# All products with v of a group in one run: a change to the order of work in an attention and experts kernel

## The chip, the cores and the metric

The kernel runs on one core of one Trainium2 chip. Times are device microseconds of one execution; the time before is the median of three runs. One core has a matrix engine (TensorE, PE in profiles), a vector engine (VectorE, DVE), a scalar engine (ScalarE, ACT), a general engine (GpSimd, POOL) and a queue that issues transfers (SyncE, SP). Each works through its own instructions in order, and they wait for each other by semaphores.

## The reference

Attention with hashed buckets, then a layer of eight experts. For 4 batches and 8 heads, 768 tokens and 64 dimensions a head:

```python
q_bits = (np.einsum('bhsd,dk->bhsk', q, proj) > 0)     # 6 bits: a token's bucket; k the same
mask = q_bucket[:, :, :, None] == k_bucket[:, :, None, :]
scores = scale * np.matmul(q, k.transpose(0, 1, 3, 2))
scores = np.where(mask, scores, -1000000000.0)
attn = softmax(scores)
x = (attn @ v), heads side by side, one row of 512 per token      # 3072 rows
expert_idx = np.argmax(x @ w_gate, axis=1)
for e in range(8):                                       # each token goes to one expert
    out[mask_e] = gate_w * (np.maximum(x[mask_e] @ w1[e], 0.0) @ w2[e])
```

All is float32. The experts' products are written as three products of rounded parts.

## The kernel before, in words

**Pairs, groups, blocks, steps.** Two heads of a batch make a pair: 16 pairs, four to a batch (`pr`, `NPAIR`). A pair has two groups (`g`) of three tiles of 128 queries. A block is one tile of queries of one head, 128 x 768 scores; a group has six, in the order of `blocks` (L522). The main loop (L773) has one step per block, 192 in all, and `n = i % 6` is the step's place in its group. I count the places as first to sixth step. Groups with `g == 0` are called even, those with `g == 1` odd.

**What a step holds.** Step i issues the scores of block i + 2 (L805: four products on TensorE into one of two score buffers, then on VectorE one pass at L241 that clips and takes the row maximum) and the exponentials of block i + 1 (ScalarE, L249 and L250). The scores of block i + 2 can start when the row maximum of block i is done, since there are two buffers.

**Two ways to turn a block.** A product with v needs the block turned. In pairs 1 to 13, the first, third and fifth block of a group go out to DRAM in pieces after the exponentials (`move`, L253: four writes, two steps later one read) and are turned by VectorE six steps later (L266, `turns`, at the very start of the step). The second, fourth and sixth block are turned by six transposes on TensorE (`transposes`, L270) into two banks of the pool `ps_t`, and two copies on ScalarE (L278) bring them to `pt`. This stands in the step after the block's own (`between`, L558).

**Products with v.** `av` (L288) is 24 products of 128 columns (12 in the program; each runs as two) for one tile of queries: both heads, six blocks of keys. For the group before (`prev`) it is called in the second, fourth and sixth step, once each (L839 and L840). After the third call ScalarE takes the sums out of PSUM (`av_evac`, L296, the copy at L300) in the next step, and two steps later `out_and_route` (L744) follows: VectorE's reciprocal (L308), three transposes on TensorE back to rows (L323) into the bank `misc` and VectorE's scaling (L324).

**Routing.** After a batch's last pair, pieces follow in the list `light`, one to a step: `logits` (L341: eight products with the gate's weights into `misc`, and a copy by ScalarE, L348), `gather_heads` (L352: three transposes into `misc`, L356, and five VectorE operations), `one_hot` (L366: five VectorE operations, those at L367 to L371 reading `misc`), `ranks` (L373: eight small products into `misc`, L376 to L381, and VectorE at L382 to L386) and `rows` (L388: two VectorE operations and three row scatters by GpSimd). This falls into the groups that begin pairs 4, 5, 8, 9, 12 and 13, and the odd ones between. The pool `ps_m` holds one bank, `misc`; it is also used by the codes of the next pair (`pair_codes`, L141, in the fourth step of an even group: eight products, L146, VectorE at L148, GpSimd at L149). Whoever writes it next waits until the last reader is done.

**Order.** `manual_schedule` (L758) keeps TensorE, VectorE, ScalarE and SP in the order in which the program issues them; `in_turn` does it for most of GpSimd's work. There is no planner: the loop's order is the order on each engine. `PREPARE` (L549) says in which step the next pair's operands are made: keys in the first step of an even group, codes and queries in the fourth, the codes' write to DRAM in the fifth; the codes come back in the first step of the odd group (L780).

**After the attention** come the experts (L921 to L1139), eight in turn, where weights are read, rounded and multiplied. The change doesn't touch them.

Of the kernel before, what the change touches and what calls it, by code (L numbers as in the profile page):

```python
# [8 lines left out]
F32 = mybir.dt.float32  # L9
# [9 lines left out]
P = 128  # L19
B, H, S, D = 4, 8, 768, 64  # L20
NB = S // P
NPAIR = H // 2
# [36 lines left out]
def lsh_attention_moe_kernel(ctx, tc, qkd, q2d, k2d, v, pjbd, wg, w1, w2, ident_in, tri_in, cols_in, eoff_in, ids_in, out):  # L59
    nc = tc.nc  # L60
    V, A, G, PE, SY = nc.vector, nc.scalar, nc.gpsimd, nc.tensor, nc.sync
# [223 lines left out]
    late = []  # L285
# [10 lines left out]
    def av_evac(pr, g, sums, o, defer):  # L296
        b, pi = divmod(pr, NPAIR)
        ot = otp.tile([P, 384], F32, name="ot")
        if defer:
            late.append(lambda: A.copy(out=ot, in_=o[:, 0:384]))  # L300
# [29 lines left out]
    def route(b, g):  # L330
# [8 lines left out]
        slot = gp.tile([P, 3, 1], I32, name="slot")  # L339

        def logits():  # L341
            lps = ps_t.tile([P, 512], F32, name="t") if (b, g) == (B - 1, 0) else ps_m.tile([P, 512], F32, name="misc")
            for pi in range(NPAIR):
                PE.matmul(out=lps[32 * pi:32 * pi + 32, 0:384], lhsT=wg_sb[:, pi, :], rhs=ots[(b, g, pi)], start=True, stop=True)
            if (b, g) == (B - 1, 0):
                V.tensor_copy(out=lsb, in_=lps[:, 0:384])
            else:
                A.copy(out=lsb, in_=lps[:, 0:384])  # L348
# [39 lines left out]
        def rows():  # L388
            x = xrows[(b, g)]
            V.reduce_max(out=slot, in_=pos, axis=AX.X)  # L390
            V.reciprocal(out=x[:, :, :, SEG + 1], in_=mx[:, :, 1:2].broadcast_to([P, 3, NG]))
            for jj in range(3):
                ins = G.indirect_dma_start(out=xs, out_offset=bass.IndirectOffsetOnAxis(ap=slot[:, jj, :], axis=0),
                                           in_=x[:, jj].rearrange("p g w -> p (g w)"), in_offset=None)
                rows_apart("xs", ins)
                if jj == 0 and b + 1 < B:
                    in_turn(ins)
            if not g and b + 1 < B:
                light.pop(0)()

        return [logits, gather_heads, one_hot, pause, ranks, rows] if b + 1 < B else [logits, gather_heads, one_hot, ranks, rows]

    def last_route(sums, o):

# [114 lines left out]
    NPR = B * NPAIR  # L519
# [26 lines left out]
    for hh in range(2):  # L546
# [2 lines left out]
    PREPARE = (  # L549
        {(0, 1): [(pair_codes, ())], (0, 2): [(codes_out, ())], (0, 3): [(k_operands, (0,))], (0, 4): [(q_operands, (0,))],  # L550
         (0, 5): [(q_operands, (1,)), (codes_back, ())], (1, 0): [(k_operands, (1,))]},
        {(0, 0): [(k_operands, (0,)), (k_operands, (1,))], (0, 3): [(pair_codes, ()), (q_operands, (0,)), (q_operands, (1,))],
         (0, 4): [(codes_out, ())]})

    def moved_block(k):
        return k % 6 in MOVES.get(steps[k][:2], ())

    def between(k):  # L558
        return 0 < k < len(steps) - 1 and moved_block(k - 1) and moved_block(k + 1)
# [18 lines left out]
    def run_expo(i):  # L578
        pr, g, jj, hh = steps[i]
        moves = moved_block(i)  # L580
        p = expo(*soft.pop(i), sums_of(pr, g), 2 * jj + hh)
        if moves:
            out, back, turn = move(p, partial(probs_t, pr, g, jj), hh)
            later.append((i, out))
            returns.append((i + 2, back))
            turns.append((i + 6, turn))
        else:
            probs[i] = p

# [16 lines left out]
    def pick_first(rows):  # L606
# [15 lines left out]
        return [counts, rows, pause, pause, pause, most, which]  # L622

    def pause():
        pass
# [118 lines left out]
    def out_and_route(pr, g):  # L744
        while divide:
            divide.pop(0)()
        if pr % NPAIR < NPAIR - 1:
            av_out(pr, g)
            return

        pieces = route(pr // NPAIR, g)
        pieces[0]()
        light.append(lambda: av_out(pr, g))
        light.extend(pieces[1:])
        if (pr, g) == (NPR - NPAIR - 1, 1):
            light.extend(pick_first(light.pop()))
# [13 lines left out]
    SY.dma_start(out=h0[0][:, 384:S], in_=q2d[0][:, 384:S])  # L770
    CLEARS = (1, 1, 2, 3, 4, 6, 8, 10)
    prev, due, extra = None, [], {}
    for i, (pr, g, jj, hh) in enumerate(steps):  # L773
        n = i % 6
        while turns and turns[0][0] == i:
            turns.pop(0)[1]()
        while later and later[0][0] <= i:
            later.pop(0)[1]()
        if (g, n) == (1, 0) and 0 < pr < NPR - 2 or (pr, g, n) == (NPR - 2, 0, 5):
# [23 lines left out]
                prefill(e)  # L803
        if i + 2 < len(steps):
            run_scores(i + 2)  # L805
        if 2 <= i < 4:
# [9 lines left out]
        while late:  # L816
            late.pop(0)()
# [4 lines left out]
        side = (g, n) == (0, 3) and 0 < pr < NPR - 1  # L822
        if due and due[0][0] == i and not last:
            due.pop(0)[1]()
        elif light and not side and (not last or n < 2):
            light.pop(0)()
        if not last:
            for f, x in PREPARE[min(pr, 1)].get((g, n), ()) if pr + 1 < NPR else ():
                f(pr + 1, *x)
        for k in (i - 1, i):  # L830
            if k in probs and (k < i or not between(k)):
                pk, gk, jk, hk = steps[k]
                transposes(probs.pop(k), probs_t(pk, gk, jk)[:, hk], (A, A))

        if prev is not None:
            if n == 0:
                o = ps_o.tile([P, 512], F32, name="o")
            order_p = blocks(prev[0], prev[1])[1]
            for jp in (order_p[:2], order_p[2:])[n] if last and n < 2 else order_p[n // 2:n // 2 + 1] if not last and n % 2 == 1 else ():  # L839
                av(prev[0], prev[1], jp, o)  # L840
            if n == (1 if last else 5):
                av_evac(prev[0], prev[1], prev[2], o, (prev[0], prev[1]) != (NPR - 2, 1) and not last)
                if not last:
# [410 lines left out]
```

## Time and profile before

| | |
|---|---|
| median of three runs | 714.4 us (709.75 to 717.0) |
| profiled execution | 719.9 us, span of its instructions 718.1 us |
| TensorE products busy | 696.8 us, 97% of the span |
| VectorE busy | 484.8 us, 68% |
| ScalarE busy | 439.1 us, 61% |
| GpSimd busy | 408.8 us, 57% |
| granted TensorE clock, mean | 0.992 |
| chain that ended last: TensorE 51%, time without a visible wait | 24% |
| pairs 1 to 13 in the profiled execution | about 33 to 356 us from the start |

How to read it: busy time of TensorE includes products that overlap, so a high share says that the engine has no holes, not that it works at its peak. A share over the whole span mixes the attention (up to about 415 us) with the experts; the stretches of single groups say more. The scores of a group start two steps ahead, so a stretch that starts with a group's first scores and ends with the next group's first scores lies two steps before the group in the program.

### The profile page before, as it was taken

How to read it: one execution, taken by the hardware profiler on the slowest of the kernel's cores; microseconds unless marked ns; L12 is line 12 of the kernel's file. 1: busy time of each engine (PE TensorE's matmuls, PEld its weight loads, DVE VectorE, ACT ScalarE, POOL GpSimd, SP SyncE). 2: the span in 40 equal slices, each digit the busy share in tenths (PEclk: the TensorE clock that was granted, in tenths of full speed). 3: DMA queues.
4: the chain of work that ended last, by engine and by line, in shares of the span. 5: the costliest groups of instructions: out<-in, count | busy, mean ns of one | idle time of the engine just before them, and what ended most of it. 6: DMA issues, size and time to landing. Idle time of an engine off the chain costs nothing.

```text
span 718.1 us, 16099 instructions
## 1 busy us (share of the span) xinstructions
PE 696.8 (97%) x5735; PEld 615.9 (86%) x5735; DVE 484.8 (68%) x1012; ACT 439.1 (61%) x996; POOL 408.8 (57%) x410
## 2 busy tenths in 40 slices
PE   7999999999999999999999989999999999999996
PEld 3888887788888888888888869999999999988994
DVE  6667878878778877878787656746464656464641
ACT  6887887788887888877777642434343434334330
POOL 3895757686656866676684320056564654707171
PEclk9999999999999999999999999999999999999999
DMA  8989878989988899799886217474746476665421
GB/s 279 294 258 283 276 232 254 290 261 278 281 260 259 250 291 266 235 289 287 230 251 185 89 62 184 118 196 119 196 135 180 145 208 160 207 163 158 147 70 47
DMA packets 110082, 150.34 MB, mean 209 GB/s; under 512 B 12548, under 2 KB 77990, under 8 KB 109992
## 3 DMA queue, kind: packets, MB, share of 16 engines
q1 hardware_dynamic: 105016, 136.52, 65.6%
q0 software_dynamic: 4976, 12.69, 5.0%
q8 instruction: 47, 0.77, 0.4%
q14 instruction: 43, 0.35, 0.1%
HBM read 94.23 MB, written 55.18 MB: 208 GB/s over the span
## 4 chain that ended last, share of the span: by engine, by line
PE 51%; issue 24%; POOL 13%; DMA 6%; DVE 2%; SPq 1%; ACT 1%; POOLq 0%; another core or an unknown queue 0%; DVEq 0%; ACTq 0%
PE o L293 17%; PE s L232 11%; POOL y L1029 11%; PE s L233 9%; PE t L275 9%; PE misc L146 2%; PE misc L323 2%; POOL yo L1027 2%; DMA y<-yo,tok 2%; DMA xr<-xs 1%; DVE p L241 1%; DMA qk<-qkd 1%; PE s L732 1%; DMA wraw<-w 1%; ACT p L250 1%
## 5 line engine op out<-in xcount | busy, mean ns | idle before, releaser
L232 PE MATMUL s<-k,q 128*128 128x512 f32 (+1 forms) x384 | 149.4, 389 | 0.1
L293 PE MATMUL o<-pt,vt 128*64 128x128 f32 x2304 | 146.8, 277 | 0.0
L293 PEld LDWEIGHTS o<-pt,vt 128*64 128x64 f32 x2304 | 123.8, 137 | 23.5 <-issue 18.4
L241 DVE TENSOR_SCALAR_CACHE_REDUCE p<-s 128x768 f32<-128x768 f32 x111 | 106.0, 955 | 35.9 <-PE s L233 31.6
L278 ACT COPY pt<-t 128x384 f32<-128x384 f32 x222 | 95.7, 482 | 52.6 <-PE t L275 46.0
L233 PE MATMUL s<-c 76*128 76x512 f32 (+1 forms) x384 | 124.1, 344 | 0.0
L1029 POOL DMA_INDIRECT y<-yo,tags x88 | 100.4, 1141 | 24.9 <-issue 22.7
L250 ACT ACTIVATE p<-p,m 128x768 f32<-128x768 f32 x111 | 104.4, 941 | 9.4 <-DVE m L244 6.7
L241 DVE TENSOR_SCALAR_CACHE_REDUCE pd<-s 128x768 f32<-128x768 f32 x81 | 76.8, 948 | 33.1 <-PE s L233 11.0
L232 PEld LDWEIGHTS s<-k,q 128*128 128x128 f32 x384 | 73.3, 191 | 27.6 <-issue 14.8
L987 ACT ACTIVATE hh<-hps 128x352 fp32r<-128x352 f32 (+3 forms) x56 | 27.9, 500 | 105.1 <-PE hps L1001 88.0
L275 PE MATMUL t<-ident,p 128*128 128x128 f32 x666 | 92.0, 274 | 0.1
L266 DVE STREAM_TRANSPOSE pt<-pq 128x768 f32<-128x768 f32 x81 | 78.6, 970 | 14.1 <-DMA pq<-moved 11.7
L701 DVE TENSOR_TENSOR wlo<-wraw,whi 128x1024 fp32r<-128x1024 f32 x60 | 72.9, 1217 | 17.4 <-ACT whi L696 15.7
L233 PEld LDWEIGHTS s<-c 76*128 76x128 f32 x384 | 74.0, 193 | 9.2 <-ACT c L208 0.4
L1020 PE MATMUL hps<-hh,whi 128*128 128x448 f32 (+9 forms) x224 | 77.3, 345 | 2.0 <-ACT whi L696 2.0
L275 PEld LDWEIGHTS t<-ident,p 128*128 128x128 f32 x666 | 75.2, 141 | 4.5 <-issue 2.5
L250 ACT ACTIVATE pd<-pd,m 128x768 f32<-128x768 f32 x81 | 75.9, 937 | 5.2 <-DVE m L244 0.8
L1020 PE MATMUL hps<-hh,wlo 128*128 128x436 f32 (+6 forms) x224 | 77.2, 344 | 1.8 <-DVE wlo L701 1.4
L1027 POOL TENSOR_TENSOR yo<-yt,tags 128x512 f32<-128x512 f32 (+3 forms) x25 | 23.2, 950 | 97.3 <-DVE yt L1022 97.2
L1020 PE MATMUL hps<-hl,whi 128*128 128x436 f32 (+6 forms) x224 | 77.1, 344 | 0.0
L1001 PE MATMUL hps<-xh,whi 128*128 128x352 f32 (+3 forms) x224 | 75.2, 336 | 0.0
(226 smaller groups left out, 1284.0 us busy)
## 6 DMA issues: line engine op xcount, KB each, us to landing
wraw<-w SPq DMA_DIRECT2D x64, 512.0 KB
moved<-pd SPq DMA_DIRECT2D x324, 96.0 KB
pq<-moved SPq DMA_DIRECT2D x81, 384.0 KB
qk<-qkd SPq DMA_DIRECT2D x30, 384.0 KB
xs<-zrow SPq DMA_DIRECT2D x8, 910.0 KB
vt<-v SPq DMA_DIRECT2D x16, 384.0 KB
coded<-cr SPq DMA_DIRECT2D x15, 192.0 KB
c<-coded SPq DMA_DIRECT2D x30, 72.0 KB
```

The costliest lines, as they stand in the source:

```text
L232: PE.matmul(out=s[:, c0:c1], lhsT=q1[:, qs], rhs=k1[:, c0:c1], start=True, stop=False)
L233: PE.matmul(out=s[:, c0:c1], lhsT=q2[0:KM, qs], rhs=k2[0:KM, c0:c1], start=False, stop=True)
L241: V.tensor_scalar(out=to, in0=of, scalar1=-0.5 * BIG, scalar2=None, op0=ALU.max, op1=ALU.max, accum_out=m[:, 0:1])
L250: A.activation(p, p, AF.Exp, bias=m[:, 1:2], scale=0.125, accum_out=sums[:, idx:idx + 1])
L266: V.transpose(out=pt()[:, hh].rearrange("p c (s j) -> p c s j", j=SQ), in_=q.rearrange("p s c i -> p c s i"))
L275: PE.transpose(out=t[:, i * P:i * P + P], in_=p[:, kc * P:kc * P + P], identity=ident)
L278: A.copy(out=dst, in_=src)
L293: PE.matmul(out=o[hh * D:hh * D + D, jj * P:jj * P + P], lhsT=vt[:, kc, hh * D:hh * D + D], rhs=pt[:, hh, kc], start=kc == 0, stop=kc == N ...
L701: loeng.tensor_tensor(out=lo[:, i:i + step], in0=cell["t"], in1=bf(hi[:, i:i + step]), op=ALU.subtract)
L1001: PE.matmul(out=hps[:, 0:w], lhsT=wt[:, c, fs], rhs=xt[:, c, 0:w], start=n == 0, stop=n == 3 * NDC - 1)
L1020: PE.matmul(out=yps[:, 0:w], lhsT=wt[:, f, ds], rhs=ht[:, 0:w], start=n == 0, stop=n == 3 * NFC - 1)
L1029: rows_apart("out", G.indirect_dma_start(out=out_seg, out_offset=bass.IndirectOffsetOnAxis(ap=tags[:, i, 0:1].bitcast(I32), axis=0), in_=y ...
```

## The change

In the groups from pair 1, first group, to pair 13, second group (`together`), the three calls of `av` for the group before all stand in the sixth step, behind that step's scores. Around that:

- The turnings on TensorE move: the second block's from the third to the fourth step, the fourth block's from the fifth step to the first of the next group, the sixth block's from the first step of the next group to its third, there in front of the step's exponentials (`turned_at`, `turn_ready`).
- VectorE turns the third block one step later, in the fourth step of the next group, behind that step's row maximum (`behind`).
- The sums leave PSUM one step later (second step instead of first).
- `pair_codes` and the queries' operands move from the fourth to the third step of an even group, the codes' write from the fifth to the fourth.
- `out_and_route` moves from the second step to the fourth. The routing pieces get fixed places (`lay_out`), counted from the step of the products with v: `logits` 3 later (third step), the scaled rows 4 (fourth), `gather_heads` 6 (sixth), `one_hot` 8 (second of the next group), `ranks` 11 (fifth), `rows` 12 (sixth). `logits` now always takes a bank of `ps_t` instead of `misc`. The steps of `pick_first`, which finds the first expert, follow 12, 16 and 17 later.

```diff
-            lps = ps_t.tile([P, 512], F32, name="t") if (b, g) == (B - 1, 0) else ps_m.tile([P, 512], F32, name="misc")
+            lps = ps_t.tile([P, 512], F32, name="t")
...
-        {(0, 0): [(k_operands, (0,)), (k_operands, (1,))], (0, 3): [(pair_codes, ()), (q_operands, (0,)), (q_operands, (1,))],
-         (0, 4): [(codes_out, ())]})
+        {(0, 0): [(k_operands, (0,)), (k_operands, (1,))], (0, 2): [(pair_codes, ()), (q_operands, (0,)), (q_operands, (1,))],
+         (0, 3): [(codes_out, ())]})
...
+    def together(pr, g):
+        return (0, 1) < (pr, g) < (NPR - 2, 0)
+
+    def turned_at(k):
+        pr, g = steps[k][:2]
+        if together(pr, g) and (pr, g) != (NPR - 3, 1):
+            return k + {1: 2, 3: 3, 5: 3}[k % 6]
+        return k + between(k)
...
-            turns.append((i + 6, turn))
+            behind = i % 6 == 2 and together(pr, g) and (pr, g) != (NPR - 3, 1)
+            turns.append((i + 6 + behind, behind, turn))
...
+    def lay_out(i, pr, g):
         if pr % NPAIR < NPAIR - 1:
-            av_out(pr, g)
+            pieces.setdefault(i + 4, []).append(lambda: out_and_route(pr, g))
             return
...
+        logits, gather_heads, one_hot, ranks, rows = route(pr // NPAIR, g)
+        way = [(3, logits), (4, lambda: out_and_route(pr, g)), (6, gather_heads), (8, one_hot), (11, ranks)]
...
+            way.append((12, rows))
+        for n, f in way:
+            pieces.setdefault(i + n, []).append(f)
...
+    def turn_ready(i):
+        for k in sorted(probs):
+            if turned_at(k) <= i:
+                pk, gk, jk, hk = steps[k]
+                transposes(probs.pop(k), probs_t(pk, gk, jk)[:, hk], (A, A))
...
             run_scores(i + 2)
+        while turns and turns[0][0] == i:
+            turns.pop(0)[2]()
...
+        if together(pr, g) and n == 2:
+            turn_ready(i)
         if i + 1 < len(steps):
             run_expo(i + 1)
...
-        for k in (i - 1, i):
-            if k in probs and (k < i or not between(k)):
-                pk, gk, jk, hk = steps[k]
-                transposes(probs.pop(k), probs_t(pk, gk, jk)[:, hk], (A, A))
+        for f in pieces.pop(i, ()):
+            f()
+        turn_ready(i)
...
+            joined = together(pr, g)
+            if n == (5 if joined else 0):
                 o = ps_o.tile([P, 512], F32, name="o")
...
+            elif joined:
+                now = order_p if n == 5 else ()
+            else:
+                now = order_p[n // 2:n // 2 + 1] if n % 2 else ()
+            for jp in now:
                 av(prev[0], prev[1], jp, o)
```

## Rows read from the trace of the kernel before

**Rows 1.** Windows: length, busy of PE, PEld, DVE, ACT, POOL, clock, DMA share, GB/s.

```profile
180.51:192.86 12.35, 12.35 (x127) 10.21 (x125) 9.98 (x19) 10.79 (x26) 7.52 (x8) 1.00 0.95 298
192.86:204.41 11.55, 11.55 (x119) 10.06 (x117) 8.86 (x18) 9.23 (x26) 7.99 (x8) 1.00 0.87 240
204.41:244.68 40.27, 39.58 (x408) 32.16 (x406) 33.01 (x84) 31.94 (x82) 26.27 (x26) 1.00 0.88 263
```

**Rows 2.** TensorE's timeline, ordinary odd group: start us, duration us, line, operation, count.

```profile
192.86 0.50 PE L232 MATMUL s<-k,q 128*128 128x512 f32 x1
...
193.68 0.82 PE L275 MATMUL t<-ident,p 128*128 128x128 f32 x6
194.25 0.48 PE L232 MATMUL s<-k,q 128*128 128x512 f32 x1
...
195.12 1.53 PE L293 MATMUL o<-pt,vt 128*64 128x128 f32 x24
196.59 0.50 PE L232 MATMUL s<-k,q 128*128 128x512 f32 x1
```

**Rows 3.** Costliest groups of instructions: count | busy us, mean ns | idle before.

```profile
L293 PE MATMUL o<-pt,vt 128*64 128x128 f32 x2304 | 146.8, 277 | 0.0
```

**Rows 4.** TensorE's timeline at the start of pair 1: scores directly behind scores.

```profile
38.29 0.40 PE L232 MATMUL s<-k,q 128*128 128x512 f32 x1
...
39.00 0.50 PE L323 MATMUL misc<-ident,ot 128*128 128x128 f32 x3
```

**Rows 5.** TensorE's timeline in a group that routes.

```profile
127.32 0.30 PE L376 MATMUL misc<-run,ident 128*128 128x24 f32 x2
...
127.61 0.86 PE L275 MATMUL t<-ident,p 128*128 128x128 f32 x6
...
129.36 0.52 PE L323 MATMUL misc<-ident,ot 128*128 128x128 f32 x3 [0.18 <-DVE mx L386]
...
132.09 0.49 PE L356 MATMUL misc<-ident,lsb 128*128 128x128 f32 x3
132.42 0.82 PE L275 MATMUL t<-ident,p 128*128 128x128 f32 x6
```

**Rows 6.** VectorE's timeline in the ordinary odd group.

```profile
193.96 0.96 DVE L241 TENSOR_SCALAR_CACHE_REDUCE pd<-s 128x768 f32<-128x768 f32 x1 [0.75 <-issue]
...
196.21 0.97 DVE L266 STREAM_TRANSPOSE pt<-pq 128x768 f32<-128x768 f32 x1
...
199.08 0.96 DVE L241 TENSOR_SCALAR_CACHE_REDUCE p<-s 128x768 f32<-128x768 f32 x1 [0.43 <-PE s L233]
...
199.96 0.18 DVE L308 RECIPROCAL inv<-sums 128x6 f32<-128x6 f32 x1
200.25 0.56 DVE L324 TENSOR_TENSOR xr<-misc,inv 128x384 f32<-128x384 f32 x1
```

**Rows 7.** TensorE's timeline in pair 14: codes, then transposes, then products with v.

```profile
366.10 0.85 PE L146 MATMUL misc<-qk,pj 128*32 128x384 f32 x8
366.88 0.88 PE L275 MATMUL t<-ident,p 128*128 128x128 f32 x6
367.69 0.55 PE L293 MATMUL o<-pt,vt 128*64 128x128 f32 x6
```

**Rows 8.** ScalarE's timeline in the ordinary odd group: two copies of a turned block.

```profile
194.21 0.86 ACT L278 COPY pt<-t 128x384 f32<-128x384 f32 x2 [1.12 <-PE t L275]
```

**Rows 9.** VectorE's timeline in two groups that route: one-hot and ranks.

```profile
122.00 0.18 DVE L367 TENSOR_TENSOR misc<-misc,mx 128x24 f32<-128x24 f32 x1
...
122.76 0.17 DVE L371 TENSOR_TENSOR lg<-misc,mx 128x24 f32<-128x24 f32 x1
...
128.48 0.18 DVE L382 TENSOR_TENSOR pos<-misc,ohb 128x24 f32<-128x24 f32 x1
...
129.06 0.16 DVE L386 TENSOR_SCALAR mx<-misc 128x3 f32<-128x3 f32 x1
```

**Rows 10.** VectorE's timeline: the longest wait for moved data.

```profile
309.62 0.98 DVE L266 STREAM_TRANSPOSE pt<-pq 128x768 f32<-128x768 f32 x1 [2.12 <-DMA pq<-moved]
```

More of the change, by code (lines that the diff above doesn't have):

```diff
@@ L294, in av, with av_evac @@
                           start=kc == 0, stop=kc == NB - 1)
-    def av_evac(pr, g, sums, o, defer):
+    def av_evac(pr, g, sums, o, defer, i):
         b, pi = divmod(pr, NPAIR)
@@ L299, in av_evac @@
         if defer:
-            late.append(lambda: A.copy(out=ot, in_=o[:, 0:384]))
+            late.append((i, lambda: A.copy(out=ot, in_=o[:, 0:384])))
         else:
@@ L397, in rows @@
                     in_turn(ins)
-            if not g and b + 1 < B:
-                light.pop(0)()
-        return [logits, gather_heads, one_hot, pause, ranks, rows] if b + 1 < B else [logits, gather_heads, one_hot, ranks, rows]
+        return [logits, gather_heads, one_hot, ranks, rows]
     def last_route(sums, o):
@@ L620, in which @@
             V.tensor_scalar(out=best_i, in0=best[:, 1:2], scalar1=-1.0, scalar2=float(E), op0=ALU.mult, op1=ALU.add)
-        return [counts, rows, pause, pause, pause, most, which]
-    def pause():
-        pass
+        return counts, most, which
     def number(tile_1):
@@ L746, in out_and_route @@
             divide.pop(0)()
+        av_out(pr, g)
+    pieces = {}
+    def lay_out(i, pr, g):
         if pr % NPAIR < NPAIR - 1:
-            av_out(pr, g)
+            pieces.setdefault(i + 4, []).append(lambda: out_and_route(pr, g))
             return
[L751 to L754, printed above, removed]
+        logits, gather_heads, one_hot, ranks, rows = route(pr // NPAIR, g)
+        way = [(3, logits), (4, lambda: out_and_route(pr, g)), (6, gather_heads), (8, one_hot), (11, ranks)]
         if (pr, g) == (NPR - NPAIR - 1, 1):
-            light.extend(pick_first(light.pop()))
+            counts, most, which = pick_first(rows)
+            way += [(12, counts), (12, rows), (16, most), (17, which)]
+        else:
+            way.append((12, rows))
+        for n, f in way:
+            pieces.setdefault(i + n, []).append(f)
     in_order.enter_context(tc.manual_schedule(engines={PE.engine, V.engine, A.engine, SY.engine}))
@@ L772, in lsh_attention_moe_kernel @@
     prev, due, extra = None, [], {}
+    def turn_ready(i):
[3 more added lines that the diff above has]
+                transposes(probs.pop(k), probs_t(pk, gk, jk)[:, hk], (A, A))
     for i, (pr, g, jj, hh) in enumerate(steps):
         n = i % 6
-        while turns and turns[0][0] == i:
-            turns.pop(0)[1]()
+        while turns and turns[0][:2] == (i, False):
+            turns.pop(0)[2]()
         while later and later[0][0] <= i:
@@ L805, in lsh_attention_moe_kernel @@
             run_scores(i + 2)
+        while turns and turns[0][0] == i:
+            turns.pop(0)[2]()
         if 2 <= i < 4:
@@ L815, in lsh_attention_moe_kernel @@
             in_turn(G.tensor_copy(out=run, in_=eoff[:, 1]))
-        while late:
-            late.pop(0)()
+        while late and late[0][0] <= i:
+            late.pop(0)[1]()
         sums = sums_of(pr, g)
@@ L821, in lsh_attention_moe_kernel @@
         last = pr == NPR - 1 and g == 1
-        side = (g, n) == (0, 3) and 0 < pr < NPR - 1
         if due and due[0][0] == i and not last:
             due.pop(0)[1]()
-        elif light and not side and (not last or n < 2):
+        elif light and (not last or n < 2):
             light.pop(0)()
@@ L829, in lsh_attention_moe_kernel @@
                 f(pr + 1, *x)
-        for k in (i - 1, i):
-            if k in probs and (k < i or not between(k)):
-                pk, gk, jk, hk = steps[k]
-                transposes(probs.pop(k), probs_t(pk, gk, jk)[:, hk], (A, A))
+        for f in pieces.pop(i, ()):
+            f()
+        turn_ready(i)
         if prev is not None:
-            if n == 0:
+            joined = together(pr, g)
+            if n == (5 if joined else 0):
                 o = ps_o.tile([P, 512], F32, name="o")
             order_p = blocks(prev[0], prev[1])[1]
-            for jp in (order_p[:2], order_p[2:])[n] if last and n < 2 else order_p[n // 2:n // 2 + 1] if not last and n % 2 == 1 else ():
+            if last:
+                now = (order_p[:2], order_p[2:])[n] if n < 2 else ()
+            elif joined:
+                now = order_p if n == 5 else ()
+            else:
+                now = order_p[n // 2:n // 2 + 1] if n % 2 else ()
+            for jp in now:
                 av(prev[0], prev[1], jp, o)
             if n == (1 if last else 5):
-                av_evac(prev[0], prev[1], prev[2], o, (prev[0], prev[1]) != (NPR - 2, 1) and not last)
-                if not last:
+                av_evac(prev[0], prev[1], prev[2], o, (prev[0], prev[1]) != (NPR - 2, 1) and not last,
+                        i + 1 + (joined and pr < NPR - 3 + (not g)))
+                if joined:
+                    lay_out(i, prev[0], prev[1])
+                elif not last:
                     due.append((i + 2, lambda a=prev[0], c=prev[1]: out_and_route(a, c)))
```

## The prediction

> **What bounds the kernel now.** I read the table of engines first: TensorE is busy for 97% of the span, so the question is whether it is the bound in the pairs that change. The windows answer it [rows 1]: in an ordinary even group (one with the codes of the next pair) TensorE is busy for 12.35 of 12.35 us, in an ordinary odd one for 11.55 of 11.55, while VectorE and ScalarE have 1.6 to 2.7 us left. The three groups after a batch's end, which route, take 40.27 us, 39.58 of them busy. So a saving on TensorE counts in full as long as nobody else comes late, and each wait put into its queue counts in full too. Then I read TensorE's timeline for what a switch costs [rows 2]. A scores run takes 0.82 us from its first product to the first transpose, 0.87 to the first product with v; six transposes take 0.57; a run with v of 24 products takes 1.47 until the next scores start. Its busy time is 1.53 and a product lasts 0.28 in the mean [rows 3], so its 24 starts are spread over about 1.26 us, 55 ns apart, and 0.21 is the way out.
>
> **The change, term by term.** All is for a group in pairs 1 to 13 (26 groups).
>
> Joining the three runs: 72 products are 71 x 0.055 + 0.21 = 4.10 us instead of 3 x 1.47 = 4.41: 0.31 less. Two entries of 0.87 become 0.82: 0.10 less. Scores directly behind scores, now in the third and the sixth step, start faster: 0.71 instead of 0.82 [rows 4], twice: 0.22 less. Nothing longer than 24 products stands in the trace; the bounds for a longer run's spacing are 55 ns and, without overlap, 0.28 us, and I take 55, the run's own. In "TensorE: Matmul & The Clock Gate", section "Back-to-back issue gap", the Trainium skill gives about 81 ns for each 128-column product that comes with its own weight load. By that the run would take 72 x 0.081 = 5.8 us, 1.7 more than by the row; the trace contradicts it for 24 in a row.
>
> An ordinary odd group is then, by steps: 0.82 + 0.57; 0.82; 0.71 + 0.57; 0.82 + 0.33 (the three transposes that bring rows back, from 132.09 to 132.42, [rows 5]) + 0.57; 0.82; 0.76; 4.10. Sum 10.89. One wait comes in: the scores of the fourth step need the bank whose row maximum starts 1.10 after its own scores [rows 2, 6], at 2.48, lasts 0.96 and frees TensorE 0.14 later from 129.06 + 0.16 to 129.36, [rows 5, 9], at 3.58 against 3.49. So 10.98, against 11.55: **0.57 less, in 10 groups**. An even one has the codes besides, now behind transposes: 0.78 for the eight products and 0.24 because transposes before such narrow products take 0.81 instead of 0.57 [rows 7]; with the fourth scores that much later, the wait of 0.09 is gone. So 11.91, against 12.35: **0.44 less, in 7 groups**. Together 5.7 + 3.1 = 8.8 us.
>
> Do the others keep up? VectorE, counted from the group's first scores: maximum at 4.66 (I take 1.08, a little under the row's 1.10, behind scores that follow transposes and start at 3.58), turning, reciprocal, scaling, turning, two maxima, turning, at 0.88 (maximum) or 0.89 (turning, 0.97 less an overlap of 0.08) each and 0.29 + 0.56 for the pair [rows 6]: done at 10.8, and the next group's first maximum starts at 10.98 + 1.10 = 12.08. So VectorE is hidden with 1.2 us to spare; the last turned block, done near 8.2, is needed by the last third of the long run near 9.4. ScalarE's 9.23 us [rows 1] fit in 10.98. SP issues the same transfers in the same order, with the codes' write one step earlier; if POOL hasn't weighed them by then, the next block's four writes queue behind it. POOL's key and query preparations and its row scatters keep their order and have 3.5 us or more of gaps [rows 1]. Those moves I cost at nothing: ScalarE still spreads the exponentials that start the transfers about evenly, and the third block's turning comes a step later than it did. If that cover is gone it is the second rival. One distance shrinks: the codes return in an odd group's first step and are read by the fifth step's scores, 7.8 us after the group's first scores until now (1.39 + 2.34 + 1.39 + 2.70), 5.3 then (3.58 + 0.82 + 0.33 + 0.57). No row shows their landing; the cost is between nothing and the whole 2.5 us in 13 pairs. TensorE never waited for them so far, so I take nothing, and count the other end to the slow side of the range.
>
> **Where it is given back: the groups that route.** The routing pieces share one PSUM bank ("misc") with the codes and with the rows' transposes, and TensorE stops at each of them until VectorE has read the last tenant. The new layout puts the pieces on TensorE next to its bare, short steps (0.82 us each), where VectorE is behind: the maximum, then the turning that now follows it, then reciprocal and scaling. From the start of the fourth step's scores, the scaling ends at 1.08 + 0.88 + 0.89 + 0.29 + 0.56 = 3.70 [rows 6], and TensorE may write the bank at 3.84.
> - First routing group (even): the logits' products, eight of the codes' shape, add 0.78, so the fourth scores start at 5.29. TensorE gets to the heads' transposes in the sixth step 3.25 us later (0.82 + 0.33 + 0.57 + 0.82 + 0.71) and waits 0.59. With 0.38 for them and 4.10 for the run: 13.61.
> - Second (odd): the logits now take a bank of the transposes. The block's transposes start at 2.92, their copies 0.53 later at the earliest (193.68 to 194.21), half of 0.86 + 0.08 for the first [rows 2, 8]: a wait of at least 0.25 past 3.73, and about 0.8 if an exponential still runs in front. ScalarE then has an exponential and the evacuation before it, so I take 0.55, between the two: logits at 4.28, fourth scores at 5.07. The ranks' products in the fifth step are reached 2.54 later, may start at 3.84: 1.30 of waiting; they take 0.29 [rows 5]. The heads' transposes in the sixth step wait for the ranks' vector work: behind the scaling stand a turning, a maximum and 0.74 of small operations [rows 9], so 3.70 - 0.08 + 0.89 + 0.88 + 0.74 + 0.14 = 6.25, against 4.95: another 1.30. With 0.38 and 4.10: 15.80.
> - Third (even): the codes wait in the third step for the one-hot work, which stands behind a maximum that starts at 2.48: 2.48 + 0.88 + 0.93 [rows 9] + 0.14 = 4.43 against 3.73, 0.70. Fourth scores 5.21, ranks 3.84 behind, 0.29, scores 0.87, run 4.10: 14.31.
>
> Sum 43.72 against 40.27: **3.45 us more per batch, three batches, 10.4 us**. Before, the same kind of wait was there but small: 0.18 us of TensorE's idle time behind the ranks [rows 5], because a run with v or transposes stood between the pieces and VectorE wasn't behind.
>
> **The sum.** -8.8 + 10.4 = +1.6 us. The profiled execution took 719.9 us (span 718.1 and 1.8 around it), so 721.5; it stands 5.5 above the median of the runs shown, 714.4, and on that median the forecast is 716.
>
> **Rivals.**
> *The pieces don't wait.* If VectorE reaches the scaling in time, the 5.74 us of waits per batch (0.59; 0.55, 1.30, 1.30; 0.70, 1.30) vanish: 716 - 17.2 = 699. Against it: the orders of TensorE and VectorE are written out, and the chain from scores to scaling holds only durations of rows. For it: the layout may let small terms overlap (VectorE's operations overlap by 0.08), and half the waits gone is 707.5. Faster by over 1% (707.3) needs half of them gone or as much found elsewhere.
> *Slower: the turnings through DRAM come too late.* The transfers take 0.95 of the DMA engines' time in the even group and 0.87 in the odd, 0.91 over a pair; 23.9 us become 22.9, so 0.95 throughout. In the trace one turning held VectorE for 2.12 us for its data [rows 10], and TensorE didn't notice, since its steps were even. In the new layout VectorE must be back for the first maximum behind the long run, with at most 1.2 us to spare, or the third scores wait. One turning as late as that in each of the 13 pairs costs 13 x 0.9 = 12 us: 728. It decides from a lateness of 1.2 us on, in the fourth or fifth step. Against it: the third block's turning got a step more, and a pair's transfers fit.
> *The long run is slower per product.* If the spacing of 55 ns held only for short runs and grew by half beyond 24, 48 products would cost 1.3 us more in 26 groups: 750. The 96 runs that make up [rows 3] show one mean, and no sign of it. By the Trainium skill's 81 ns, in the section named above, all 72 would be that slow, and the kernel near 760.
>
> **How the numbers follow.** The forecast 0.48, no waits of the pieces (or under half) 0.24, late turnings 0.26, a slow long run 0.02. What a measurement of this kernel can tell from no change is about 1%: 707.3 to 721.5. The forecast's own range is 711 to 721; the second case reaches from 699 to 707, the third from 722 to 730. For eight in ten I go from 703 to 727, which leaves out the far half of the fast case and the ends of the slow ones. Faster 0.24, same 0.48, slower 0.28.
>
> **What would show it.** Right: ordinary groups of about 11.0 and 11.9 us; one TensorE run with v of 72 products; routing groups near 13.6, 15.8 and 14.3, with TensorE idle in front of the ranks' and the heads' products, ended by the scaling or by the ranks' vector work. Wrong: no such idle time (first rival); VectorE waiting for moved data with the scores late behind it (second); products with v further apart than 55 ns (third).

## The result and the profile after

The changed kernel takes 722.9 us (median of four runs, 720.5 to 725.4) against 714.9 us: ratio 1.0131, 95% interval 1.0094 to 1.0168. It is 1.3% slower. Its profiled execution took 720.5 us, with a span of 718.7.

The spans of the two profiled executions are nearly equal only because the one of before took some 8 us longer behind the groups measured here, mostly among the experts, which the change doesn't touch (317 us against 309). The attention, measured up to the first step of its last group (pair 15, odd), comes 8.8 us later, 410.0 us against 401.2, and this agrees with the medians. A group is measured here from the scores that its own first step issues to those that the next group's first step issues; [rows 1] begin two steps earlier, which changes the lengths by 0.02 us at most. In us:

| groups | before | after | difference | forecast |
|---|---|---|---|---|
| 10 odd ordinary | 115.7 | 111.8 | -3.9 | -5.7 |
| 7 even ordinary | 85.7 | 85.0 | -0.7 | -3.1 |
| 3 first that route | 40.5 | 40.9 | +0.4 | +0.3 |
| 3 second that route | 40.1 | 52.6 | **+12.5** | +7.4 |
| 3 third that route | 40.4 | 42.2 | +1.8 | +2.6 |
| after pair 13, up to pair 15's odd group | 41.4 | 40.4 | -1.0 | 0 |
| sum | | | +9.0 | +1.5 |

The 0.2 us between the sum and the 8.8 lie in front of pair 1.

These are the windows of the changed kernel that answer to [rows 1], with the same columns: an undisturbed even group, an odd one, and the three that route.

```profile
187.48:199.43 11.95, 11.95 (x127) 10.20 (x125) 9.93 (x19) 9.72 (x26) 11.32 (x11) 1.00 0.86 263
199.43:210.32 10.89, 10.89 (x119) 10.04 (x118) 8.13 (x17) 9.47 (x26) 4.20 (x6) 1.00 0.96 295
210.32:254.76 44.44, 39.54 (x407) 32.44 (x405) 33.70 (x86) 30.66 (x82) 30.75 (x29) 1.00 0.81 240
```

The ordinary groups came out as worked out (11.91 and 10.98). In the routing ones TensorE's work is the same 39.5 us as before, and 4.9 us of holes have opened where 0.7 were. TensorE's timeline of the odd group, for [rows 2], and the page's row of the products, for [rows 3]:

```profile
200.25 0.82 PE L275 MATMUL t<-ident,p 128*128 128x128 f32 x6
...
206.24 4.15 PE L293 MATMUL o<-pt,vt 128*64 128x128 f32 x72
210.32 0.50 PE L232 MATMUL s<-k,q 128*128 128x512 f32 x1
```

```profile
L293 PE MATMUL o<-pt,vt 128*64 128x128 f32 x2304 | 139.3, 278 | 1.0 <-issue 0.9
```

The 72 products go through in one run; 4.08 us lie between its first start and the next scores (forecast 4.10). Now the second routing group of pair 8, TensorE's timeline; the brackets give the idle time and who ended it:

```profile
227.87 0.85 PE L344 MATMUL t<-ot,wg_sb 128*32 128x384 f32 x8 [0.45 <-ACT pt L278]
...
232.41 0.40 PE L376 MATMUL misc<-run,ident 128*128 128x24 f32 x2 [1.08 <-DVE xr L324]
...
234.90 0.52 PE L356 MATMUL misc<-ident,lsb 128*128 128x128 f32 x3 [1.14 <-DVE mx L386]
235.35 4.06 PE L293 MATMUL o<-pt,vt 128*64 128x128 f32 x65
239.63 0.54 PE L293 MATMUL o<-pt,vt 128*64 128x128 f32 x5 [0.23 <-issue]
240.36 0.42 PE L293 MATMUL o<-pt,vt 128*64 128x128 f32 x2 [0.19 <-issue]
```

The three forecast waits are all there, in front of the logits, the ranks and the heads. Those of the first and the third routing group are there too, here in pairs 4 and 5:

```profile
116.38 0.55 PE L356 MATMUL misc<-ident,lsb 128*128 128x128 f32 x3 [0.37 <-DVE xr L324]
...
143.71 0.85 PE L146 MATMUL misc<-qk,pj 128*32 128x384 f32 x8 [0.53 <-DVE lg L371]
...
148.15 0.40 PE L376 MATMUL misc<-run,ident 128*128 128x24 f32 x2 [0.88 <-DVE xr L324]
```

What was not forecast is the run behind the waits of the second group: its 72 starts are spread over 5.16 us here, 5.18 in pair 12 and 6.32 in pair 4, where every ordinary run takes 3.88. In pair 4 most of it runs at half the clock; in pairs 8 and 12 the clock is full and the end of the run pauses three times. Windows of pair 4's group:

```profile
120.94:131.00 10.06, 8.52 (x63) 6.71 (x61) 7.62 (x19) 7.73 (x21) 0.81 (x2) 1.00 0.87 241
131.00:138.00 7.00, 5.87 (x51) 5.57 (x53) 4.04 (x16) 2.46 (x6) 3.72 (x5) 0.51 0.99 320
```

And a disturbed ordinary group, pair 10's even one, written (10, even) from here on, 12.68 us long: first VectorE, which waits for a moved block in front of the group's first row maximum, then TensorE, whose third scores wait for that row maximum, since they need its score buffer.

```profile
266.56 0.98 DVE L266 STREAM_TRANSPOSE pt<-pq 128x768 f32<-128x768 f32 x1 [2.14 <-DMA pq<-moved]
267.46 0.92 DVE L241 TENSOR_SCALAR_CACHE_REDUCE pd<-s 128x768 f32<-128x768 f32 x1
```

```profile
268.45 0.50 PE L232 MATMUL s<-k,q 128*128 128x512 f32 x1 [0.49 <-DVE pd L241]
```

Waits of that length were there before too. The one of [rows 10] was not the longest: it stood in a group of 13.62 us, whose two like took 13.45, so it cost 0.17 us at most, and one of 2.24 us in (11, even) cost nothing (12.33 us, like the other even groups). Four ordinary groups are too long like this or, in (1, odd), mostly through late codes: 3.2 us in all over 10.89 and 11.92. Below I call this sum the ordinary groups' excess; it leaves out (13, odd), behind which the order goes back to the old one.

### The profile page after: what moved, and what is told of

Read it like the earlier page. It is cut to its first block, busy times and chain, and to the rows that moved or that the text cites. A ratio compares the mean times of both kernels' runs of the same rounds, so it can differ in the third digit from the quotient of the medians.

```text
span 718.7 us, 16081 instructions
## 1 busy us (share of the span) xinstructions
PE 686.2 (95%) x5735; PEld 615.6 (86%) x5735; DVE 482.8 (67%) x1012; ACT 431.6 (60%) x996; POOL 415.0 (58%) x410
## 4 chain that ended last, share of the span: by engine, by line
issue 20%; POOL 14%; PE 11%; DMA 3%; DVE 1%; ACT 1%; SPq 1%; POOLq 0%; another core or an unknown queue 0%; DVEq 0%; ACTq 0%
POOL y L1060 12%; PE o L293 4%; PE t L275 2%; POOL yo L1058 2%; PE s L232 2%; DMA y<-yo,tok 2%; PE s L233 1%; DMA xr<-xs 1%; PE s L737 1%; DMA xs<-xr,slot 0%; PE misc L323 0%; POOL tags L977 0%; SPq L662 0%; POOLq L1060 0%
## 5 line engine op out<-in xcount | busy, mean ns | idle before, releaser
L232 PE MATMUL s<-k,q 128*128 128x512 f32 (+1 forms) x384 | 143.4, 378 | 1.6 <-DVE pd L241 1.4
L293 PE MATMUL o<-pt,vt 128*64 128x128 f32 x2304 | 139.3, 278 | 1.0 <-issue 0.9
L293 PEld LDWEIGHTS o<-pt,vt 128*64 128x64 f32 x2304 | 127.6, 139 | 9.0 <-issue 5.3
L1060 POOL DMA_INDIRECT y<-yo,tags x88 | 105.6, 1200 | 24.9 <-issue 22.6
L266 DVE STREAM_TRANSPOSE pt<-pq 128x768 f32<-128x768 f32 x81 | 78.6, 970 | 16.7 <-DMA pq<-moved 13.6
L233 PEld LDWEIGHTS s<-c 76*128 76x128 f32 x384 | 73.7, 192 | 10.7 <-issue 1.4
L1051 PE MATMUL hps<-hh,whi 128*128 128x448 f32 (+9 forms) x224 | 75.7, 338 | 0.0
L1051 PE MATMUL hps<-hl,whi 128*128 128x436 f32 (+6 forms) x224 | 75.6, 338 | 0.0
L1051 PE MATMUL hps<-hh,wlo 128*128 128x436 f32 (+6 forms) x224 | 75.6, 338 | 0.0
L1032 PE MATMUL hps<-xl,whi 128*128 128x428 f32 (+6 forms) x224 | 74.9, 335 | 0.0
```

What stands on the lines that cost most here:

```text
L232: PE.matmul(out=s[:, c0:c1], lhsT=q1[:, qs], rhs=k1[:, c0:c1], start=True, stop=False)
L233: PE.matmul(out=s[:, c0:c1], lhsT=q2[0:KM, qs], rhs=k2[0:KM, c0:c1], start=False, stop=True)
L266: V.transpose(out=pt()[:, hh].rearrange("p c (s j) -> p c s j", j=SQ), in_=q.rearrange("p s c i -> p c s i"))
L1032: PE.matmul(out=hps[:, 0:w], lhsT=wt[:, c, fs], rhs=xt[:, c, 0:w], start=n == 0, stop=n == 3 * NDC - 1)
L1051: PE.matmul(out=yps[:, 0:w], lhsT=wt[:, f, ds], rhs=ht[:, 0:w], start=n == 0, stop=n == 3 * NFC - 1)
L1060: rows_apart("out", G.indirect_dma_start(out=out_seg, out_offset=bass.IndirectOffsetOnAxis(ap=tags[:, i, 0:1].bitcast(I32), axis=0), in_=y ...
```

## The experiments

Ratios are to the kernel before, run beside each set on the same chip (707.8, 715.3 and 708.7 us); the median times of different sets don't compare, the ratios and the profiles' group lengths do. The diffs show the lines that matter; ... marks a cut.

**Without the routing groups.** These keep the order of before.

```diff
-        return (0, 1) < (pr, g) < (NPR - 2, 0)
+        return (0, 1) < (pr, g) < (NPR - 2, 0) and not (pr >= NPAIR and 2 * (pr % NPAIR) + g < 3)
...
+        if together(pr, g) and (pr, g) != (NPR - 3, 1):
+            return k + {1: 2, 3: 3, 5: 1}[k % 6]
```

> The joined run and its layout stay in the groups that don't route; the groups that route (the first three of pairs 4, 8 and 12 on) have the order of the kernel before, with the codes where they were. If the routing groups take back what the ordinary ones give (my theory), this is the gain alone: odd ordinary groups 0.7 us and even ones 0.4 us shorter, less some 0.6 us in each of three new transitions, so 710 to 713 us, and the routing groups are back at 13.4 us each. If the joined run costs something everywhere (late turnings and codes, the transfers), the time stays at 718 us or above with routing groups of 13.4 us.

Measured: 1.0013 (0.9984 to 1.0041), 709.1 us against 707.8. The 1.3% are gone, so the loss sits in the routing groups. But the gain isn't there either: the undisturbed ordinary groups take 10.89 and 11.92, and others lose it again, 7.1 us over those lengths in all (the groups beside a change of order left out), most in (10, even), 15.79 us long. There TensorE waited 2.15 us for a row maximum, and behind the wait the granted clock fell to 0.50. Its VectorE, in front of that row maximum:

```profile
260.98 0.98 DVE L266 STREAM_TRANSPOSE pt<-pq 128x768 f32<-128x768 f32 x1 [3.95 <-DMA pq<-moved]
```

The three returns to the old order cost 1.2 us each in the first routing group. The expectation of 710 to 713 on a base of 714.9, 2 to 5 us of gain, missed.

**Ranks behind the run.**

```diff
-        way = [(3, logits), (4, lambda: out_and_route(pr, g)), (6, gather_heads), (8, one_hot), (11, ranks)]
+        way = [(3, logits), (4, lambda: out_and_route(pr, g)), (6, gather_heads), (6, one_hot), (13, ranks)]
-            way.append((12, rows))
+            way.append((14, rows))
```

> In the changed kernel, the one-hot work moves two steps earlier (behind the heads' work, beside the long run), the ranks two steps later (first step of the next group, behind the long run) and the rows with them. Theory of the waits: the ranks' waits of about 1.1 and 0.9 us in the second and third routing group, the heads' wait of 1.1 in the second and the codes' of 0.5 in the third go; per batch 3.6 less, 10.8 in all: 712 us, and if the second group's slow long run (5.1 us over three batches beyond its waits) hangs on them or on the scatters beside it, 707. If TensorE only waits elsewhere instead (VectorE is simply behind in those groups), the second routing group stays above 15.5 us and the time above 718.

Measured: 0.9956 (0.9926 to 0.9986), 3.1 us under the kernel before. The three second routing groups take 13.26 us each instead of 17.0 to 18.5, and the starts of every run in them are spread over 3.88 us. TensorE in pair 8:

```profile
228.22 0.55 PE L356 MATMUL misc<-ident,lsb 128*128 128x128 f32 x3 [0.37 <-DVE xr L324]
228.69 4.15 PE L293 MATMUL o<-pt,vt 128*64 128x128 f32 x72
```

The nine routing groups are 18.4 us shorter than in the changed kernel, and the attention ends 11.4 us earlier: 5.2 us were given back in ordinary groups and 2.2 behind pair 13.

**Only the scatters later.**

```diff
-            way.append((12, rows))
+            way.append((13, rows))
```

> In the changed kernel, only the rows' step (two operations on VectorE and three row scatters by GpSimd) goes one step later, out of the step with the long run; the ranks and all waits of TensorE stay. If the scatters beside it make the long run of the second routing group slow, its 72 starts spread over 3.9 us again instead of 5.2 to 6.3 and the time falls by 3 to 5 us to about 718 to 720. If the waits in front of the run make it slow, or what it reads, nothing changes: 722 to 724, spread 5 us or more.

Measured: 1.0106 (1.0060 to 1.0152), some 2 us better than the change's 1.0131, less than the 3 to 5 expected and within the intervals. The waits stay (1.08 and 1.13 us). In pairs 8 and 12 the run's spread is back at 3.88 and the group at 15.72, which the forecast gave as 15.80; TensorE in pair 8:

```profile
233.17 0.52 PE L356 MATMUL misc<-ident,lsb 128*128 128x128 f32 x3 [1.13 <-DVE mx L386]
233.62 4.15 PE L293 MATMUL o<-pt,vt 128*64 128x128 f32 x72
```

In pair 4 the clock falls again (mean 0.56 and 0.59 in the four microseconds from 132) and the run takes 5.54. So two effects lay behind one symptom: pauses, which went away in both groups at full clock when the rows' step moved (three scatters and two short operations of VectorE), and the clock, which didn't.

**All three edits**: ranks later and one-hot earlier, as above, and VectorE's turning behind the pieces.

```diff
-        while turns and turns[0][0] == i:
-            turns.pop(0)[2]()
         if 2 <= i < 4:
...
         for f in pieces.pop(i, ()):
             f()
+        while turns and turns[0][0] == i:
+            turns.pop(0)[2]()
```

> As the kernel with the later ranks, and VectorE's turning of the third block stands behind the pieces of its step instead of in front of them, so that the scaling comes 0.9 us earlier. Theory of the waits: besides, the first routing group's wait of 0.4 to 0.6 us before the heads goes: 1.2 to 1.8 us less than the kernel with the later ranks, so 705.5 to 711 us, which is below the kernel before (714.9). If VectorE is simply behind in those groups, the wait moves to the long run's last third or to the next scores and nothing is gained against the kernel with the later ranks.

Measured: 0.9935 (0.9915 to 0.9955), 702.6 us against 707.8. The first routing groups fall from 13.39 to 12.80, and the nine are 20.4 us shorter than in the changed kernel and 5.7 shorter than before. The ordinary groups' excess is 8.0 us.

**The turning behind the pieces, alone.** The diff above, on the changed kernel.

> The changed kernel with one edit: VectorE's turning of the third block stands behind the pieces of its step (the scaling) instead of between the row maximum and them. Theory of the waits: the scaling ends 0.9 us earlier, so the first routing group loses its wait before the heads (0.4 to 0.6), the third its wait before the ranks (0.9 to 0.2); in the second the ranks' wait shrinks likewise, but the heads wait for the ranks' vector work, which ends where it did, so that wait grows by the same. 1.3 us less per batch, 3.9 in all, ratio to the kernel before about 1.008 instead of 1.013. If the scaling isn't what TensorE waits for, the groups keep 13.4 and 14.05 us.

Measured: 1.0097 (1.0059 to 1.0135). First groups 12.79 (0.60 less), third 13.19 (0.87 less): as expected. In the second the heads' wait grew from 1.14 to 2.0, as expected too, and then the clock fell in all three batches, where it had fallen in one. TensorE in pair 4, then windows of pair 8 (its wait ends near 235):

```profile
132.27 0.87 PE L356 MATMUL misc<-ident,lsb 128*128 128x128 f32 x3 [2.00 <-DVE mx L386]
133.08 6.70 PE L293 MATMUL o<-pt,vt 128*64 128x128 f32 x72
```

```profile
234.00:236.00 2.00, 0.93 (x5) 0.63 (x7) 1.86 (x11) 1.41 (x4) 0.00 (x0) 0.50 0.94 297
236.00:238.00 2.00, 2.00 (x20) 2.00 (x22) 1.16 (x6) 1.05 (x3) 1.40 (x2) 0.50 0.93 306
```

**Fewer transfers.**

```diff
+        if pr > 2:
+            return [raws[(pr % 2, hh)]]
...
+        if pr > 2:
+            return vts[pr % 2]
```

> The changed kernel without the loads of queries, keys and v from pair 3 on (about 1.15 of the 5.8 MB that a pair moves); the later pairs compute with the data of pairs 1 and 2, so the output is theirs. Theory of late transfers: the ordinary groups that were too long in the changed kernel (in its profile 3.2 us over their 10.89 and 11.92: late turned blocks and late codes) come down to under 1 us in all, and if the transfers also disturb the second routing group's long run, its spread is 3.9 us in pairs 8 and 12; the waits of the pieces stay, with routing groups of 13.4, 15.7 and 14.1 us. In all 3 to 7 us below the changed kernel. If the lateness doesn't come from the transfers' load, the ordinary groups keep 3 us or more.

Measured: the whole time (919.9 us) says nothing, since other data send other tokens to the experts; the attention does. The DMA engines' share falls from 0.88 to 0.78 between 60 and 340 us, and from pair 3 on every ordinary group but (13, odd) takes 10.84 to 10.89 or 11.93 to 11.94; the excess of 1.4 us lies in pairs 1 and 2, which still have their loads. The changed kernel first, then this one:

```profile
60.00:340.00 280.00, 266.19 (x2760) 229.98 (x2758) 215.74 (x473) 217.25 (x570) 182.32 (x177) 0.99 0.88 263
```

```profile
60.00:340.00 280.00, 267.19 (x2786) 231.44 (x2782) 216.27 (x471) 216.09 (x569) 184.39 (x180) 0.99 0.78 219
```

So the loads made the blocks of pairs 3 to 12 late. By which way this run doesn't tell: they take the DMA engines' time, and they also stand in SyncE's queue. Of that queue only the wait for the codes' weighing is ruled out, as it stayed (13.7 us, 10.1 in the changed kernel). The second routing groups keep 17.4, 17.4 and 17.1 us, twice at half clock and once with the pauses: neither comes from the sum of the transfers.

**Every turning behind**, on the kernel with all three edits.

```diff
-            behind = i % 6 == 2 and together(pr, g) and (pr, g) != (NPR - 3, 1)
-            turns.append((i + 6 + behind, behind, turn))
+            behind = together(pr, g) and (pr, g) != (NPR - 3, 1)
+            turns.append((i + 6 + (behind and i % 6 == 2), behind, turn))
```

> On the kernel with all three edits, VectorE's turnings of the first and the fifth block stand behind the row maximum and the pieces of their step too, so that a late block no longer holds the row maximum and the scores behind it. Theory of late transfers: the ordinary groups' excess (8.0 us in the profile of the kernel with all three edits) falls to under half, 4 us less in the time (ratio to the kernel before about 0.988). If VectorE has no slack to give back, or the three buffers for the turned blocks come free too late for the next reads, the excess stays at 8 us or grows.

Measured: 0.9916 (0.9888 to 0.9944), 709.3 us against 715.3. From pair 2 on the even ordinary groups are all between 11.96 and 11.99. But each odd group has at least 0.38 more in its third step (11.27), as the first block's turning now separates two row maxima, so that the excess stays at 7.6 us, and one run in pair 13 lost 2.5 us waiting for the fifth block. The page's rows of the turning, before, after, and here; behind the bar busy and mean, then the idle time in front and what ended most of it:

```profile
L266 DVE STREAM_TRANSPOSE pt<-pq 128x768 f32<-128x768 f32 x81 | 78.6, 970 | 14.1 <-DMA pq<-moved 11.7
```

```profile
L266 DVE STREAM_TRANSPOSE pt<-pq 128x768 f32<-128x768 f32 x81 | 78.6, 970 | 16.7 <-DMA pq<-moved 13.6
```

```profile
L266 DVE STREAM_TRANSPOSE pt<-pq 128x768 f32<-128x768 f32 x81 | 78.6, 971 | 0.4 <-DMA pq<-moved 0.4
```

VectorE waited nearly as long for the blocks before (11.7 us) as after (13.6). So most of the lateness isn't the change's; it took away what had hidden it.

**The codes' write a step later**, on the kernel with all three edits.

```diff
-         (0, 3): [(codes_out, ())]})
+         (0, 4): [(codes_out, ())]})
```

> On the kernel with all three edits, the codes' write goes back to the fifth step of the even group. In that kernel's profile SyncE's queue waits 13.5 us in 7 places for GpSimd to weigh the codes, and the next block's four writes stand behind it. If this makes the turned blocks late, the wait goes and the ordinary groups' excess of 8.0 us falls by 2 to 4. If the transfers are late from their load alone, the excess stays, and the scores of the odd groups' fifth step wait longer for the codes (2.6 us in 3 places there): no gain or up to 3 us more.

Measured: 1.0008 (0.9981 to 1.0035), so worse than the 0.9935 it started from. SP's wait for the weighing went (13.5 us to nothing), but SP then waits 10.7 us for the codes themselves, and the blocks stay late (17.1 us of VectorE's time). The ordinary groups' excess grew from 8.0 to 14.4 us. Of that 6.5 lie in (1, odd), where TensorE waited 3.0 us and the clock fell, so the loss of some 5 us is more than the 3 that I had allowed for. SyncE's wait for the codes, in us, times and longest:

```profile
SPq L180 <- DMA coded<-cr: 10.7, 10, 1.7
```

**The scatters one by one**, on the kernel with all three edits.

```diff
...
+        way += [(14 + 2 * jj, f) for jj, f in enumerate(spread)]
...
```

> On the kernel with all three edits, the three row scatters of a routing group go out one by one, two steps apart, instead of together. In that kernel's profile the four ordinary groups right behind the routing ones (5,1), (6,0), (9,1) and (10,0) are 4.4 us too long together, with turned blocks late. If the burst of 0.8 MB makes them late, these fall to under 2 us. If it is the sum of the bytes, the lateness moves to the groups behind and the time stays within 1 us of the kernel with all three edits.

Measured: 1.0090 (1.0056 to 1.0124). It failed by a cause of its own: the last scatter holds one of the three buffers for rows, and VectorE's scaling stops for it, with the turnings and the long run behind.

```profile
160.65 0.56 DVE L324 TENSOR_TENSOR xr<-misc,inv 128x384 f32<-128x384 f32 x1 [8.01 <-DMA xs<-xr,slot]
```

```profile
162.15 0.69 PE L293 MATMUL o<-pt,vt 128*64 128x128 f32 x2 [4.78 <-DVE pt L266]
```

It doesn't decide whether the burst makes blocks late.

**The first block's turning behind**, on the kernel with all three edits: one step later in odd groups and in the same step in even ones (the diff); then in even groups alone.

```diff
+            behind = i % 6 < 4 and together(pr, g) and (pr, g) != (NPR - 3, 1)
+            turns.append((i + 6 + (behind and (i % 6 == 2 or not g)), behind, turn))
```

> On the kernel with all three edits: the turning of a group's first block goes behind the row maximum, in even groups' successors (odd groups) one step later, in odd groups' successors (even groups) in the same step; the fifth block's stays in front. In the kernel with every turning behind, even groups had no excess left (before: up to 1.5 us where the first block was late), but each odd group lost 0.38 in its third step, since the first block's turning stood between its first two row maxima. Theory: with the turning behind the second maximum that loss goes and the gain stays: ordinary excess 2 to 4 us, ratio to the kernel before 0.986 to 0.990. If one step later is too late for the buffers or for the third maximum, odd groups lose 0.4 or more elsewhere and the ratio stays at 0.992 or above.

> As the kernel before it, but the odd groups turn the first block in front of the first maximum as the kernel with all three edits does; only in even groups it stands behind. Theory: odd groups at 10.89 us without the 0.38, exposed to late blocks again; even groups without excess: ratio 0.988 to 0.992.

Measured: 0.9923 (0.9899 to 0.9947) and 0.9936 (0.9914 to 0.9957). The odd groups lose 0.2 instead of 0.4, but excess remained (11.1 and 8.1 us), and both ratios lie above their ranges. So far the order of the turnings has only moved where a late block strikes. Five versions beat both kernels, with overlapping intervals; the lowest ratio is that of every turning behind, 0.9916.

## Why the prediction was right or wrong

The range, 703 to 727, held the time; the forecast of 716 was 7 us low, and the case it called likeliest (within 1%) isn't the one that came. The time lies where the second rival had put it (722 to 730), but by chance: late blocks cost 2.5 us, not 12, and the rest has other causes. Step by step:

- **The run's price: right.** 55 ns for each of 72 products: 3.88 us from the first start to the last. The rival of a slower long run falls. The Trainium skill ("TensorE: Matmul & The Clock Gate", section "Back-to-back issue gap") gives about 81 ns for a 128-column product in a stream of products that load their weights; the undisturbed runs of 72 here show 55.
- **Ordinary groups: right where undisturbed** (10.89 for 10.98, 11.92 for 11.91), **wrong as a sum**, -4.6 for -8.8. Late blocks and codes took 3.2 us, and the last odd group, behind which the order goes back to the old one, got 0.9 longer instead of 0.6 shorter; no run tests why.
- **Where it failed: "Those moves I cost at nothing".** I had the cover right (1.2 us of VectorE's slack) and named the rival, but made it all or nothing. The trace of before held 10.2 us of waits for moved blocks over the ordinary and routing groups, in 12 places; I looked at one alone, and not at the longest. Each wait over the new slack costs about its rest: in front of a group's first row maximum, waits of 1.30, 1.97, 1.98 and 2.14 us made their groups 0.30, 0.73, 0.71 and 0.76 longer, 2.5 us in all. Without the loads the excess from pair 3 on was gone, so they are shown to cause it there.
- **The codes' return at nothing**: late once, 1.08 us of TensorE's time; small as it stands.
- **The waits of the pieces: right, and the main reason.** 0.59; 0.55, 1.30, 1.30; 0.70, 1.30 were forecast, 0.37; 0.45, 1.08, 1.14; 0.53, 0.88 were measured, and the groups took 13.39, 15.72 (where the run was undisturbed) and 14.05 us for 13.61, 15.80 and 14.31. Moving the ranks took the second group's two long waits away (13.26 us; 0.45 in front of the logits and 0.37 in front of the heads are left), and moving one turning changed the first and third by about the amounts worked out. The first rival (no waits) is out.
- **What the sum lacked: the run behind the waits.** Its starts were spread over 6.32, 5.16 and 5.18 us instead of 3.88, 5.0 us more over three batches. It is the larger part of the miss (+9.0 for +1.5).

What that last part is, the runs settle halfway. Half clock, in the second routing groups: it came in or behind a single wait of 2.0 us three times out of three, with two waits of about 1.1 us four times out of nine, and never once these waits were gone. Pauses at full clock came three times, each with scatters beside the run; in the two runs at full clock without scatters there were none. So in these groups the clock needs the waits, and the pauses, as far as five runs can tell, need the rows' step. But scatters alone don't make them: in fourteen other runs that had scatters start beside them the spread was 3.88 to 4.05 us. In the kernel with the codes' later write three odd groups paused (5.4 us), with waits of 0.3 to 0.45 somewhere in front, and with every turning behind two paused once each (4.25 and 4.49 us). What else a pause needs, with no semaphore in sight, stays open.

That the five better versions stop at 0.992 to 0.996, when their routing groups alone are 18 us or more shorter than the changed kernel's, has probably the same reason as the ordinary shortfall: the transfers stay the same while the time for them shrinks, and blocks and codes come late for it. This is argued and not shown, as none of the five was run with fewer transfers.

## What to carry to other kernels

Joining TensorE's short runs saves what the switches cost, but it also makes the steps uneven, and whatever used to be spread between the runs (a shared bank's readers, a vector chain, a transfer) must now fit into the short ones. Before such a change, list every wait that costs nothing now, with its length, and subtract the new slack from each, not only from the longest. Small pieces that wait for a vector engine belong behind the long run, where that engine has caught up, and not in front of it.

## What the runs showed of the hardware

- A stop of TensorE can cost more than its length: in or behind a wait of 2.0 us in the second routing groups the granted clock fell to 0.50, the lower level (1.2 GHz), three times out of three, and the starts of the run of 72 products were spread over 5.5 to 6.4 us instead of 3.88, though the engine was busy throughout. Elsewhere waits of about that length went either way: the clock fell with 2.15 us (without the routing groups, (10, even)) and 1.92 us (first block's turning behind, (5, odd)), and stayed at 1.00 with 2.48 us (every turning behind, (13, odd)) and 1.88 us (first block's turning behind, (10, even)).
- Of the runs of 72 products at full clock that had row scatters by GpSimd start beside them, fourteen were undisturbed (spread 3.88 to 4.05 us), six were 1.3 to 1.6 us longer and two 0.4 and 0.6, mostly with idle time put down to issue. What tells them apart is open.
- Taking a sixth of the transfers away (263 to 219 GB/s, DMA share 0.88 to 0.78) brought VectorE's waits for moved blocks from 13.1 us down to 4.1, none of them above 1.1 us, and the ordinary groups of pairs 3 to 12 lost nothing to them any more.
